# A fused attention and gated-MLP block: a new order for the first rows, maxima stored by ScalarE's queue, score tiles taken in turn, and scratch of q and k in two parts

## The chip, the cores and the metric

The kernel runs on one core of a Trainium2 chip. A core has five engines that run side by side, each with its own queue of instructions: TensorE (PE in the profile, its weight loads are PEld), VectorE (DVE), ScalarE (ACT), GpSimd (POOL) and SyncE (SP), which here only issues transfers (DMAs) between the chip's memory and SBUF. SP, ACT and POOL can all issue DMAs. Products go to PSUM, from which DVE and ACT read. The metric is the time of one execution in microseconds on the device; the kernel before took 1966.16 us (median of 3 runs, 1964.69 to 1969.37).

## The reference

With x of 2048 rows and 512 columns, all in float32:

```python
xn = layernorm(x)
qkv = xn @ wqkv                       # 32 heads of 16 columns
p = softmax(q @ k.T * 16 ** -0.5)     # for each head, 2048 x 2048
A = (p @ v) @ wo
z = gelu(xn @ w_in)                   # 2048 x 1792
z1, z2 = z[:, :896], layernorm(z[:, 896:])
B = (z1 * (w_sp @ z2 + b_sp)) @ w_out
out = x + A + B
```

## The kernel before

**Numbers in two parts.** Most operands are split into a high part (a copy in the type that PE reads at full rate, `F32R`) and a low part (the difference). `mm3` (L161) makes a product of three: high by high, low by high, high by low. `split` (L157) makes the parts of a psum tile, with a copy on ACT and a difference on DVE. `end` (L182) does so for weights: early weights get their high part by a second DMA that POOL issues (`begin`, L168, `early`) and the low part on DVE; later ones get both on POOL.

**The start** (L816 to L854). `load_x` (L223) loads four tiles of 128 rows of x as two transfers. `norm_x` (L233) normalises them: statistics on DVE, root and scaled copy on ACT. `turn_x` (L255) turns a group of four tiles with 16 transposes on PE into four column blocks, each in a psum tile of its own from `spsum` (L153), splits them and stores them to `xscr`. Then, for each of four groups of 512 rows, `qk_group` (L287) makes q and k of the first eight heads (m = 0, 12 products each), and `v_tile` (L334) makes v for four tiles, 12 products each. Between the v tiles, the next group is turned and the one after it normalised.

**Scratch of q and k.** The scores of a head use three products stacked in rows of one: q's parts high, low, high against k's high, high, low, each 16 rows. `qk_split` (L305) makes the parts of a projection; `qk_store` (L278) writes them to `qscr` or `kscr`, which hold three parts: one transfer of two parts (512 KB) and one of the repeated high part (256 KB). `load_stacks` (L598) then reads for a pair of heads the 48 rows of each head and side in one transfer, into `qst` and `kst`. The tile `hl` that the stores read has three buffers (L147). `store` goes by POOL's queue at the start and by SP's later (L134).

**The loop** (L943 to L1014). A step is one block of 128 keys for a pair of heads and 512 queries. A period of two half-steps has three steps. In each half-step the code writes, in order, the products of score tiles (`scores`, L898, for a step) and of maximum tiles (`max_mm`, L622, 27 steps ahead), the exponentials on ACT (`exp`, L920), the products with v (`pv`, L864), the maxima on DVE (`max_red`, L632), and pieces of the other work (the remaining q and k, then the MLP and the output), which generators hand out by a credit in PE time and estimated loads of the engines. Engines run what is written in that order. Score and maximum tiles both come from `spsum`: a ring of three psum buffers of two banks.

**The maxima.** Every 16 steps, `max_fin` (L640) ends a group: five small operations on DVE, the last a transpose into `ms`; then SP stores `ms` to `mscr` a half-step later (L659), and two half-steps later SP reads it back as four rows into `qst`, where it becomes a part of the scores' product. `later` (L125) puts a call off by so many half-steps; `flush` makes those that are due.

**The output of the MLP.** `mlp_out` (L565) loads for each tile of rows two pieces of the gated activation and one tile of x, one tile ahead.

Of the kernel before, what the change touches and what calls it, by code (L numbers as in the profile page):

```python
# [16 lines left out]
P = 128  # L17
# [3 lines left out]
DH = 16  # L21
# [10 lines left out]
RING = 20  # L32
LEAD = 27
# [6 lines left out]
def fused_block(ctx, tc, x, wqkv, wo, w_in, w_spT, b_sp, w_out, out):  # L40
# [39 lines left out]
    qscr = [dr.tile([P, 3, S], F32, name=f"qscr{m}") for m in range(4)]  # L80
    kscr = [dr.tile([P, 3, S], F32, name=f"kscr{m}") for m in range(4)]
# [45 lines left out]

    def flush():
        due = [l for l in late if l[0] <= now[0]]
        late[:] = [l for l in late if l[0] > now[0]]  # L130
        for _, fn, args in due:
            fn(*args)
# [19 lines left out]

    def spsum(nm):  # L153

        return ps.tile([P, 2, 512], F32, tag="s", name=nm, bufs=3)
# [12 lines left out]
    def begin(nm, src, n, blocks=1, t=None, early=None):  # L168
# [4 lines left out]
        dst, hi = rw[:, :n], t[:, 0, :n]  # L173
        if blocks > 1:
            src = src.rearrange("(c p) f -> p c f", p=P)
            dst, hi = (v.rearrange("p (c f) -> p c f", c=blocks) for v in (dst, hi))
        move(dst, src)
        if early:
            nc.gpsimd.dma_start(hi, src)
        return t, rw, n  # L180

    def end(loaded, early=False):  # L182
        t, rw, n = loaded
        if early:
            nc.vector.tensor_sub(t[:, 1, :n], rw[:, :n], t[:, 0, :n].bitcast(F32))
# [37 lines left out]
    def load_x(g):  # L223
        xt = [at.tile([P, 2, D], F32, tag="pf", name=f"x{g}_{i}", bufs=PF) for i in (0, 2)]
        for i in range(len(xt)):
            k = 4 // len(xt)
            t = 4 * g + k * i
            rows = x[t * P:(t + k) * P, :]
            move(xt[i], rows if k == 1 else rows.rearrange("(a p) d -> p a d", p=P))
            for j in range(k):  # L230
                xs[g, k * i + j] = xt[i] if k == 1 else xt[i][:, j, :]

    def norm_x(g, parts=1):  # L233
# [5 lines left out]
        for a in range(parts):  # L239
            tiles = range(a * k, (a + 1) * k)  # L240
            sl = slice(a * k, (a + 1) * k)
# [13 lines left out]
    def turn_x(g):  # L255
        for c in range(ND):
            pt = spsum(f"xT{g}_{c}")[:, 0, :]
            for i in range(4):
                nc.tensor.transpose(pt[:, i * P:(i + 1) * P], xs[g, i][:, c * P:(c + 1) * P], ident)
            t = piece(f"xnT{g}_{c}")  # L260
            split(t[:, 0, :], t[:, 1, :], pt, 512)
            store(xscr[g][c], t)
            xnT[g, c] = t
# [13 lines left out]

    def qk_store(scr, order, hl, sl, first=False):  # L278
        put = move if first else store
        r = 1 if order[0] == order[1] else 0  # L280
        put(scr[:, r:r + 2, sl], hl)
        put(scr[:, 2 - 2 * r, sl], hl[:, 0, :])
# [22 lines left out]
    def qk_split(m, g, a, src):  # L305
        hl = hilo(f"qkhl{m}_{a}_{g}")
        act(hl[:, 0, :], src, AF.Copy, 512)
        yield
        if m:
            gps(1.3).tensor_sub(hl[:, 1, :], src, hl[:, 0, :].bitcast(F32))  # L310
            yield from pool_done()
        else:
            dve(512).tensor_sub(hl[:, 1, :], src, hl[:, 0, :].bitcast(F32))
        qk_store((qscr, kscr)[a][m], ((0, 1, 0), (0, 0, 1))[a], hl, slice(g * 512, (g + 1) * 512), m == 0)
# [19 lines left out]
    def v_tile(t, ws):  # L334
        acc = dpsum(f"v{t}", "do"[t % 2])
        sl = slice((t % 4) * P, (t % 4 + 1) * P)
        for c in range(ND):
            xt = xnT[t // 4, c]
# [226 lines left out]
    def mlp_out():  # L565
        def load(t):
            hp = []
            for i, n in enumerate((4, 3)):
                h = piece(f"hp{t}_{i}")
                move(h[:, :, :n * P].rearrange("p a (f q) -> p a f q", q=P), hscr[t // 4][:, :, t % 4, 4 * i:4 * i + n, :])  # L570
                hp.append(h)
            xt = t512(f"xr{t}")
            move(xt, x[t * P:(t + 1) * P, :])
# [24 lines left out]
    def load_stacks(p, cols=slice(0, S)):  # L598
# [3 lines left out]
        for j in range(2):  # L602
            for i, (t, scr) in enumerate(((q, qscr), (k, kscr))):
                args = t[64 * j:64 * j + KS, cols], scr[m][sl[j], :, cols]
                if p and 2 * j + i:
                    later(2 * j + i, move, *args)
                else:
                    move(*args)
# [3 lines left out]
    NSTEP = NP * 64  # L612
    mstep = {}
# [26 lines left out]
    def max_fin(i):  # L640
# [18 lines left out]
        later(1, move, mscr[g % 4].rearrange("b k x -> (b k) x"), ms)  # L659
# [155 lines left out]
    with tc.manual_schedule(engines=engines):  # L815
        load_x(0)  # L816
        w0 = [begin(*qk_weights(0, a), early="t") for a in range(2)]
        load_x(1)
# [234 lines left out]
```

## Time and profile before

| | |
|---|---|
| median of 3 runs | 1966.16 us |
| lowest and highest | 1964.69, 1969.37 us |
| profiled execution | 1965.23 us, of which the span of instructions is 1963.1 us |
| PE busy | 1933.9 us (99%) |
| DVE busy | 1372.9 us (70%) |
| ACT busy | 1231.7 us (63%) |
| POOL busy | 720.9 us (37%) |
| scores, products with v, maxima (PE) | 445.6, 511.0, 446.9 us |
| maxima on DVE | 1024 of 1.222 us |
| exponentials on ACT | 1024 of 1.025 us |
| memory traffic | 190.09 MB read, 101.97 MB written |

The span runs from the first instruction to the last. PE's busy time is a model: products are pipelined, so where it says 99%, PE may still lose time between them. The table of a stretch gives, for each engine, busy time and the number of instructions in it. A timeline's line gives start, duration, engine, line of the code, operation, output and inputs, and in brackets how long the engine stood idle before and what ended that. DMA time is not shown on an engine; the queue that issues it is (SPq, POOLq).

### The profile page before, as it was taken

Reading aid. Unit: us, or ns where it says so; the run is one execution under the profiler, and the core shown is the slowest. Engines: PE = TensorE matmul, PEld = TensorE weight load, DVE = VectorE, ACT = ScalarE, POOL = GpSimd, SP = SyncE. Lnnn points to the kernel's source line nnn. Section 1 sums busy time; section 2 is a strip of 40 time slices with the busy share of each in tenths; the row PEclk is TensorE's granted clock in tenths of the full one; section 3 lists DMA queues with packets and bytes.
Section 4 is the critical chain, followed back from the end, with each engine's and each line's share of the span. In section 5 each row is a group of like instructions: output and inputs, shape, how many; then the busy total and the mean of one; then the engine's idle time right before and its main releaser. Section 6 shows DMA issues by size and latency. Waiting matters only on the chain.

```text
span 1963.1 us, 32545 instructions
## 1 busy us (share of the span) xinstructions
PE 1933.9 (99%) x12544; PEld 1047.0 (53%) x12544; DVE 1372.9 (70%) x1562; ACT 1231.7 (63%) x1402; POOL 720.9 (37%) x787
## 2 busy tenths in 40 slices
PE   7999999999999999999999999999999999999998
PEld 6765555555555555555555555555555555555543
DVE  5256777777777677777777777777777777777872
ACT  4336778888777665656666665665566655556664
POOL 2234368789776931026122531017112300002100
PEclk9999999999999999999999999999999999999999
DMA  9586444363535645365545744346364645355323
GB/s 327 204 292 200 139 107 122 108 176 111 154 117 159 187 123 140 91 162 159 151 138 154 211 129 125 108 126 204 105 163 135 176 142 145 106 152 154 105 73 113
DMA packets 234195, 294.20 MB, mean 150 GB/s; under 512 B 34536, under 2 KB 134520, under 8 KB 231160
## 3 DMA queue, kind: packets, MB, share of 16 engines
q1 hardware_dynamic: 229816, 282.08, 49.4%
q0 software_dynamic: 4224, 10.04, 1.4%
q8 instruction: 99, 1.62, 0.3%
q14 instruction: 56, 0.46, 0.1%
HBM read 190.09 MB, written 101.97 MB: 149 GB/s over the span
## 4 chain that ended last, share of the span: by engine, by line
PE 91%; DVE 3%; POOL 2%; DMA 2%; ACT 1%; issue 1%; SPq 0%; DVEq 0%; POOLq 0%; ACTq 0%
PE o L877 23%; PE mx L630 15%; PE st L903 15%; PE sp L162 7%; PE sp L164 5%; PE sp L163 5%; PE mo L162 2%; PE z1p L162 2%; PE qk L162 1%; DVE mm L638 1%; PE mo L163 1%; PE mo L164 1%; PE z2p L162 1%; PE z1p L164 1%; PE z1p L163 1%; PE qk L163 1%
## 5 line engine op out<-in xcount | busy, mean ns | idle before, releaser
L638 DVE TENSOR_REDUCE mm<-mx 128x2 f32<-128x1024 f32 x1024 | 1221.5, 1222 | 501.3 <-PE mx L630 497.2
L57 ACT ACTIVATE pf<-st 128x1024 f32<-128x1024 f32 x1024 | 1028.7, 1025 | 621.9 <-PE st L903 597.2
L877 PE MATMUL o<-pf,vall 128*32 128x512 f32 (+1 forms) x5120 | 511.0, 513 | 0.0
L630 PE MATMUL mx<-kst,qst 48*128 48x512 f32 x2048 | 446.9, 434 | 3.1 <-DVE mm L638 2.0
L903 PE MATMUL st<-qst,kst 50*128 50x512 f32 x2048 | 445.6, 432 | 1.5 <-DVE mm L638 1.4
L630 PEld LDWEIGHTS mx<-kst,qst 48*128 48x128 f32 x2048 | 192.0, 185 | 268.7 <-ACT pf L57 168.6
L903 PEld LDWEIGHTS st<-qst,kst 50*128 50x128 f32 x2048 | 193.3, 185 | 164.0 <-issue 85.7
L877 PEld LDWEIGHTS o<-pf,vall 128*32 128x32 f32 x5120 | 131.4, 109 | 233.7 <-issue 211.7
L162 PE MATMUL sp<-wsp,zs 128*128 128x512 f32 x448 | 193.8, 433 | 0.3 <-DVE z1i L549 0.2
L556 POOL TENSOR_TENSOR z1i<-z1i,hhl 128x512 f32<-128x512 f32 x28 | 36.0, 1286 | 425.9 <-DVE z1i L549 422.4
L164 PE MATMUL sp<-wsp,zs 128*128 128x512 f32 x448 | 175.9, 393 | 0.0
L163 PE MATMUL sp<-wsp,zs 128*128 128x512 f32 x448 | 175.9, 393 | 0.0
L162 PEld LDWEIGHTS sp<-wsp,zs 128*128 128x128 f32 x448 | 83.9, 187 | 68.9 <-issue 52.1
L164 PEld LDWEIGHTS sp<-wsp,zs 128*128 128x128 f32 x448 | 84.1, 188 | 19.3
L163 PEld LDWEIGHTS sp<-wsp,zs 128*128 128x128 f32 x448 | 84.4, 188 | 12.2
L187 POOL CAST wo<-wo0r 128x512 fp32r<-128x512 f32 x1 | 0.6, 611 | 191.4 <-DMA wo0r<-in_wo 191.4
L310 POOL TENSOR_TENSOR qkhl<-qr,qkhl 128x512 fp32r<-128x512 f32 x24 | 30.9, 1289 | 78.9 <-ACT qkhl L57 78.8
L162 PE MATMUL z2p<-w,xt 128*128 128x448 f32 x128 | 51.3, 401 | 0.0
L162 PE MATMUL mo<-wout,hp 128*128 128x512 f32 x112 | 48.5, 433 | 0.6 <-DVE xr L593 0.4
L691 POOL TENSOR_TENSOR ob<-ob 128x512 f32<-128x512 f32 (+1 forms) x16 | 20.6, 1288 | 77.0 <-DMA ob<-rscr 54.5
L164 PE MATMUL z2p<-w,xt 128*128 128x448 f32 x128 | 46.9, 366 | 0.0
L163 PE MATMUL z2p<-w,xt 128*128 128x448 f32 x128 | 46.8, 365 | 0.0
(378 smaller groups left out, 1974.8 us busy)
## 6 DMA issues: line engine op xcount, KB each, us to landing
zs<-z2scr SPq DMA_DIRECT2D x112, 512.0 KB
escr<-e SPq DMA_DIRECT2D x60, 256.0 KB
hscr<-hhl SPq DMA_DIRECT2D x28, 512.0 KB
qst<-qscr SPq DMA_DIRECT2D x30, 384.0 KB
kst<-kscr SPq DMA_DIRECT2D x30, 384.0 KB
xscr<-xnT POOLq DMA_DIRECT2D x16, 512.0 KB, 6.0
qscr<-qkhl SPq DMA_DIRECT2D x16, 512.0 KB
kscr<-qkhl SPq DMA_DIRECT2D x16, 512.0 KB
```

Source lines behind the costliest of these rows:

```text
L57: return nc.scalar.activation(out, in_, func, **kw)
L162: nc.tensor.matmul(acc, lh, rh, start=first, stop=False)
L163: nc.tensor.matmul(acc, ll, rh, start=False, stop=False)
L164: nc.tensor.matmul(acc, lh, rl, start=False, stop=last)
L187: gps(0.6).tensor_copy(t[:, 0, :n], rw[:, :n])
L310: gps(1.3).tensor_sub(hl[:, 1, :], src, hl[:, 0, :].bitcast(F32))
L556: gps(1.3).tensor_add(z1, z1, hl[:, 1, :].bitcast(F32))
L630: nc.tensor.matmul(acc[:, j, :], qst[p % 2][rows, tt * P:(tt + 1) * P], kst[p % 2][rows, kc * 512:(kc + 1) * 512], start=True, stop=True)
L638: dve(1024).tensor_reduce(mmax[i // 16][:, :, t, kc], mstep.pop(i), AX.X, ALU.max)
L691: gps(1.3).tensor_mul(both[rows, 0, :], both[rows, 0, :], both[rows, 2, :])
L877: nc.tensor.matmul(acc[cols:cols + VW, a:a + w], vpack(kt - 1 + r, 2 * p + j), pf[:, j * 512 + a:j * 512 + a + w], start=(kt == 1 and a == ...
L903: nc.tensor.matmul(st[:, j, :], kst[p % 2][rows, kt * P:(kt + 1) * P], qst[p % 2][rows, c * 512:(c + 1) * 512], start=True, stop=True)
```

## The change

- **Start.** x's first group comes as four transfers, two tiles first, then the four blocks of v's weights, then the other two tiles, then the weights of q and k. The second DMAs of early weights are gone: POOL casts the high parts of v's weights, DVE makes three low parts and POOL the fourth; POOL makes both parts of the first weights of q and k. A group's turning can be done for two tiles of four: the first two tiles are turned, v is made for them, then the other two, v again, and only then q and k of this group. All of a group's transposes are written first, into three psum tiles of which one holds two column blocks, and the splits behind them. ACT takes a root of a constant before anything else. Fifteen products of zeros (`WARM`) are written on PE ahead of all others. Group 1 is normalised between the v tiles of group 0 and turned between its q and its k.
- **Maxima.** The store of `ms` is put in a list, `behind`, and issued by ACT's queue at the end of the next half-step, behind its exponentials.
- **Score tiles.** `spsum` takes three tiles with one buffer each in turn, where it had one tag with three buffers.
- **Scratch.** `qscr` and `kscr` hold two parts. For k the order of the parts is low, high. One store writes both; `load_stacks` reads the two parts as 32 rows and the high part again as 16 rows, eight transfers where there were four.
- **Output of the MLP.** From the second tile on, the three loads are put off by one, two and three half-steps.

```diff
-    qscr = [dr.tile([P, 3, S], F32, name=f"qscr{m}") for m in range(4)]
-    kscr = [dr.tile([P, 3, S], F32, name=f"kscr{m}") for m in range(4)]
+    qscr = [dr.tile([P, 2, S], F32, name=f"qscr{m}") for m in range(4)]
+    kscr = [dr.tile([P, 2, S], F32, name=f"kscr{m}") for m in range(4)]
...
+    def soon(k, fn, *args):
+        fn(*args)
+
...
     def spsum(nm):
-        return ps.tile([P, 2, 512], F32, tag="s", name=nm, bufs=3)
+        turns[0] += 1
+        return ps.tile([P, 2, 512], F32, tag=f"s{turns[0] % 3}", name=nm, bufs=1)
...
-    def end(loaded, early=False):
+    def end(loaded, low=None, high=False):
         t, rw, n = loaded
-        if early:
-            nc.vector.tensor_sub(t[:, 1, :n], rw[:, :n], t[:, 0, :n].bitcast(F32))
+        if high:
+            low.tensor_sub(t[:, 1, :n], rw[:, :n], t[:, 0, :n].bitcast(F32))
+        elif low:
+            nc.scalar.activation(t[:, 0, :n], rw[:, :n], AF.Copy)
+            low.tensor_sub(t[:, 1, :n], rw[:, :n], t[:, 0, :n].bitcast(F32))
         else:
             gps(0.6).tensor_copy(t[:, 0, :n], rw[:, :n])
...
-    def turn_x(g):
+    def turn_x(g, lo=0, hi=4):
+        tiles = [spsum(f"xT{g}_{lo}_{c}") for c in range(3)]
+        sl = slice(lo * P, hi * P)
         for c in range(ND):
-            pt = spsum(f"xT{g}_{c}")[:, 0, :]
-            for i in range(4):
-                nc.tensor.transpose(pt[:, i * P:(i + 1) * P], xs[g, i][:, c * P:(c + 1) * P], ident)
-            t = piece(f"xnT{g}_{c}")
-            split(t[:, 0, :], t[:, 1, :], pt, 512)
-            store(xscr[g][c], t)
-            xnT[g, c] = t
+            for i in range(lo, hi):
+                nc.tensor.transpose(tiles[c % 3][:, c // 3, i * P:(i + 1) * P], xs[g, i][:, c * P:(c + 1) * P], ident)
+        for c in range(ND):
+            if lo == 0:
+                xnT[g, c] = piece(f"xnT{g}_{c}")
+            t = xnT[g, c]
+            split(t[:, 0, sl], t[:, 1, sl], tiles[c % 3][:, c // 3, sl], (hi - lo) * P)
+            if hi == 4:
+                store(xscr[g][c], t)
...
-    def qk_store(scr, order, hl, sl, first=False):
-        put = move if first else store
-        r = 1 if order[0] == order[1] else 0
-        put(scr[:, r:r + 2, sl], hl)
-        put(scr[:, 2 - 2 * r, sl], hl[:, 0, :])
...
-        qk_store((qscr, kscr)[a][m], ((0, 1, 0), (0, 0, 1))[a], hl, slice(g * 512, (g + 1) * 512), m == 0)
+        (store if m else move)((qscr, kscr)[a][m][:, :, g * 512:(g + 1) * 512], hl)
...
-                move(h[:, :, :n * P].rearrange("p a (f q) -> p a f q", q=P), hscr[t // 4][:, :, t % 4, 4 * i:4 * i + n, :])
+                (later if t else soon)(i + 1, move, h[:, :, :n * P].rearrange("p a (f q) -> p a f q", q=P), hscr[t // 4][:, :, t % 4, 4 * i:4 * i + n, :])
...
-            move(xt, x[t * P:(t + 1) * P, :])
+            (later if t else soon)(3, move, xt, x[t * P:(t + 1) * P, :])
...
-                args = t[64 * j:64 * j + KS, cols], scr[m][sl[j], :, cols]
-                if p and 2 * j + i:
-                    later(2 * j + i, move, *args)
-                else:
-                    move(*args)
+                two = t[64 * j:64 * j + 2 * DH, cols], scr[m][sl[j], :, cols]
+                one = t[64 * j + 2 * DH:64 * j + KS, cols], scr[m][sl[j], i, cols]
+                for args in (two, one):
+                    if p and 2 * j + i:
+                        later(2 * j + i, move, *args)
+                    else:
+                        move(*args)
...
-        later(1, move, mscr[g % 4].rearrange("b k x -> (b k) x"), ms)
+        behind.append((now[0] + 1, mscr[g % 4].rearrange("b k x -> (b k) x"), ms))
...
+        nc.scalar.activation(mhalf, epst, AF.Sqrt)
+        idle = piece("idle")
+        nc.vector.memset(idle.bitcast(F32)[:, 0, :], 0.0)
+        nc.vector.memset(mhalf, -0.5)
+        rest = dpsum("idle", "o")
+        for _ in range(WARM):
+            nc.tensor.matmul(rest, idle[:, 0, 0:P], idle[:, 0, :], start=True, stop=True)
...
+        for t, rw, n in wv:
+            nc.gpsimd.tensor_copy(t[:, 0, :], rw)
+        norm = norm_x(0, 2)
+        next(norm)
+        next(norm)
+        wv = [end(l, (nc.vector, nc.gpsimd)[c == 3], True) for c, l in enumerate(wv)]
+        turn_x(0, 0, 2)
+        next(norm)
...
+        w0 = [end(l) for l in w0]
+        run(norm)
+        v_tile(0, wv)
+        v_tile(1, wv)
+        turn_x(0, 2, 4)
+        norm1 = norm_x(1, 2)
+        next(norm1)
+        v_tile(2, wv)
+        next(norm1)
+        next(norm1)
+        v_tile(3, wv)
+        run(norm1)
...
             for n in ns[1:]:
                 exp(n)
+            while behind and behind[0][0] <= half:
+                nc.scalar.dma_start(*behind.pop(0)[1:])
```

## The prediction

> **What bounds the kernel now.** I read the page's busy shares first, then busy time by stretch, then the timeline of the first 14 us and of one step in the main loop.
>
> ```profile
> PE 1933.9 (99%) x12544; PEld 1047.0 (53%) x12544; DVE 1372.9 (70%) x1562; ACT 1231.7 (63%) x1402; POOL 720.9 (37%) x787
> ```
>
> PE is the bound; a change that adds no matmul to its crowded part can gain only where PE stands idle. Where is that? By stretch (columns: busy time and count of PE, PEld, DVE, ACT, POOL; granted clock; DMA share; GB/s):
>
> ```profile
> 0.00:13.90 13.90, 4.38 (x17) 3.42 (x18) 6.94 (x21) 6.71 (x10) 6.68 (x16) 1.00 1.02 294
> 13.90:88.00 74.10, 72.10 (x339) 58.97 (x337) 27.15 (x58) 30.11 (x53) 14.17 (x24) 1.00 0.76 281
> 88.00:143.90 55.90, 53.48 (x234) 36.80 (x232) 32.71 (x32) 18.40 (x30) 24.94 (x22) 1.00 0.71 256
> 143.90:146.90 3.00, 1.92 (x13) 0.97 (x12) 1.58 (x2) 2.40 (x3) 0.06 (x1) 1.00 0.96 354
> 146.90:150.40 3.50, 3.50 (x12) 2.29 (x12) 2.00 (x2) 1.57 (x3) 1.29 (x1) 0.52 0.35 132
> 150.40:1900.00 1749.60, 1745.79 (x11564) 921.08 (x11564) 1280.25 (x1422) 1140.44 (x1270) 672.85 (x723) 1.00 0.50 142
> 1900.00:1963.10 63.10, 52.73 (x380) 23.45 (x372) 22.23 (x28) 32.04 (x36) 0.92 (x2) 0.94 0.26 89
> ```
>
> Of 29.2 us idle, 9.5 lie before 13.9, 2.0 in the projections, 3.5 between 88 and 147, 3.8 in the whole loop, and 10.4 in the tail, which the change leaves alone. At 146.9 to 150.4 the clock is half: a stall costs twice. The start in detail:
>
> ```profile
> 4.54 0.69 DVE L244 BATCH_NORM_STATS2 bst<-x 128x6 f32<-128x512 f32 x1 [3.46 <-DMA x<-in_x]
> ...
> 7.01 1.52 ACT L253 ACTIVATE x<-x,rs 128x512 f32<-128x512 f32 x2 [0.43 <-DVE rs L249]
> ...
> 9.34 1.52 ACT L253 ACTIVATE x<-x,rs 128x512 f32<-128x512 f32 x2 [0.43 <-DVE rs L249]
> ...
> 10.91 3.04 PE L259 MATMUL xT<-ident,x 128*128 128x128 f32 x13 [0.23 <-ACT x L253]
> ...
> 13.60 0.63 PE L162 MATMUL qk<-xnT,wqk 128*128 128x512 f32 x1
> ```
>
> The first product waits for all four tiles of x to be normalised and turned. The thirteen transposes follow each other every 0.213 us (2.56 us over twelve steps). Later ones take half of that:
>
> ```profile
> 44.39 1.47 PE L259 MATMUL xT<-ident,x 128*128 128x128 f32 x12
> 46.45 0.66 PE L259 MATMUL xT<-ident,x 128*128 128x128 f32 x4 [0.59 <-DVE xnT L159]
> ```
>
> Twelve in 1.47 us, the last lasting 0.27: 0.109 us apart. The last four wait for a psum buffer that VectorE still reads.
>
> **The change, part by part.** I sum against the profiled execution: 1965.23 us (span 1963.1), 0.93 under the median of 1966.16.
>
> *Start.* Now: 12 products at 0.2267 us make a group of 2.72 us; the first maximum is at 87.76, and 13.60 + 0.24 (first product late) + 24 groups (65.3) + 48 transposes (5.2) + about 3.4 of gaps comes to 87.7. After the change x comes tile by tile, the value weights next, and a product needs two tiles only. Two tiles of x are the 512 KB of the first old transfer (statistics at 4.54 at the latest; the first tile half a transfer earlier, about 3.9). Statistics 0.69 and 0.66 with aggregates, root, reciprocal and offset took 2.47 from 4.54 to ACT's 7.01; from 3.9 that gives 6.4, and 1.52 more is 7.9. The added root on ACT (0.30 behind the table load that ends at 2.00) and VectorE's memset behind it are done by 2.5, under the wait for x. Eight transposes at 0.109 follow. The split is now of 256 columns: ACT between 512 (0.60) and 256 (0.39 in the tail's 256-column copies), VectorE about 0.42 (0.425 for its 256-column copy). The first product comes 0.52 + 0.39 after 7.9 (0.52 is 10.91 to 11.43), at 8.8, its second one 0.42 later: in effect a stream from 9.0. The weights: six transfers of 0.26 MB at 294 to 380 GB/s land by 5.3 to 6.2; POOL's casts (0.61 x 4) end by 8 and VectorE's three differences (0.69 each) by 9, before each is used. So the stream starts 13.84 - 9.0 = 4.8 us earlier.
>
> Against that: the other eight transposes of the group now stand in the stream (0.87), and the third tile's first products wait for their split (0.55: ACT first empties v1, 0.60, then 0.39 and 0.42). The turning of groups 1 to 3 loses its gaps, since four half tiles lie in three buffers: 0.28 + 0.54 at 25 to 27.5, 0.59 at 46.45, the same again at 65: 2.0, and 0.13 us for each restart. Inserting group 1's transposes after the first q group may wait 0.3 for its last normalised tile. Start, net: 4.8 - 0.87 - 0.55 - 0.3 + 2.0 + 0.4 + the small early stall at 19.46 (0.15) = 5.6; bounds 3.5 (weights or x later by 2) and 7.3 (first x as early as 3.4, no waits).
>
> *The products of zeros.* Fifteen of 512 columns start when a 128x512 memset is done (about 1.6). At the half-clock spacing of 0.427 (147.53 to 149.24) they end at 8.0, at 0.227 at 5.0: before the transposes, or 0.1 into them. They buy the clock for 8 + 8 transposes and the first products.
>
> **A rule for the clock.** The row: after 2.6 us of transposes the product at 14.07 is already followed at 0.23, and after stops of 1.55 and 1.08 us within ten us the clock halves for 3.4 us. The Trainium skill (TensorE: Matmul & The Clock Gate, Part 1: The HAM clock gate) says that the array runs at half rate until a window of about 3.4 us, free-running, has been busy, and falls back after an idle one. The halved rows agree with it; by it the zeros (busy from 1.6 for 3.4 to 6.4 us) do open the gate, but whether it stays open over the pause before 7.9 depends on where the window lies, which is a rival below. The page's Part 4 says that transposes do not open the gate; 10.91 to 14.07 speaks against it.
>
> *q and k scratch.* 32 stores of 256 KB go (32 issues of about 0.45 on SP); each stack load becomes two, 4 more issues of 0.42 for each of 19 loads of stacks (76 x 0.42 = 32 us of SP's queue). SP is idle for hundreds of us in waits, and a stack is asked for over 40 us ahead; no PE wait on a stack shows. The bytes read stay. What it frees is the stretch where the stores hold up PE:
>
> ```profile
> 136.18 0.63 ACT L57 ACTIVATE qkhl<-qr 128x512 fp32r<-128x512 f32 x1 [7.16 <-DMA kscr<-qkhl]
> ...
> 137.35 0.50 PE L162 MATMUL qk<-xnT__1182,wqk 128*128 128x512 f32 x1 [1.55 <-ACT qr L57]
> ```
>
> ACT waits for a buffer whose two stores (768 KB, DMA share 1.05) are not done. Five stores in flight lose a third, 1.3 MB or 3.3 us at 400 GB/s: I take the 1.55 as gone. What is late next is the maximum at 146.00 (1.08, VectorE); I leave that and the halved 3.4 us (worth 1.7) in place. So 1.5; bounds 0 and 1.55 + 1.08 + 1.7 = 4.3.
>
> *Maxima by ACT's queue.* 64 issues leave SP (0.33 each) and wait on ACT for VectorE's transpose, behind the odd half-step's exponential:
>
> ```profile
> 1012.10 0.21 DVE L657 STREAM_TRANSPOSE ms<-mrow 128x32 f32<-128x32 f32 x1
> ...
> 1012.75 1.02 ACT L57 ACTIVATE pf<-st 128x1024 f32<-128x1024 f32 x1 [0.63 <-PE st L903]
> 1015.67 1.02 ACT L57 ACTIVATE pf<-st 128x1024 f32<-128x1024 f32 x1 [1.90 <-PE st L903]
> ```
>
> The transpose ends at 1012.31, the exponential at 1013.77, ACT then rests until 1015.67. Read group by group, the transpose has ended first in all 63 groups of the loop, and in 54 ACT then rests 0.56 us or more; in the other nine another ACT piece of the MLP follows and comes 0.33 later. No trace shows an issue on ACT: between SP's 0.33 and POOL's 0.57 (cscr). I take 0.4, hidden by that rest; on the path 0, bounds -1 (SP's queue moves sooner) and +9 x 0.57 = 5. Queued behind it on ACT are the next exponentials, which PE needs one half-step (2.7 us) later. The store lands some 1.5 us later, against 12 steps or 22 us until its rows are read.
>
> *Score tiles in turn.* At 1006.86 and 1007.55 the waits already are those of a ring taken in turn (first maximum after the first exponential, second after the second). Worth 0; bounds -3.8 (all of the loop's idle time) and +1.
>
> *Late loads of the output stage.* One half-step to three later (2.7 to 8 us) against 14 us between load (1615.80) and first use (1631.34): 0.
>
> Sum: 5.6 + 1.5 = 7.1, so 1965.2 - 7.1 = 1958.1, or 1959 from the median. I say 1958.5.
>
> **Rivals.**
> Middle freed: the earlier stores also clear the 146.00 stall, and with it the halved clock: 2.8 more, and with the first x at 3.4 another 0.5: 1955. For it: both stalls lie 9 us apart in one chain of ACT. Against: the second is a wait for VectorE's maxima.
> Cold again: the gate closes in the pause after the zeros, so 16 transposes cost 0.10 more each and up to 3.4 us of products half their speed (1.7), or x comes at 4.5: 3.3 lost, 1962. For: stops of 1.1 to 1.6 did it at 147. Against: the stop at 135.7 to 137.35 alone did not.
> Slower: ACT's queue. If an issue is not 0.4 but waits for ACT's pipeline or for the transpose, the following exponential and then PE's maximum that takes its buffer come late. From 7.1 / 63 = 0.11 us per group on PE's path the gain is gone; at 0.2 us it is 1971, and at 0.33 (every issue fully exposed, 21 us) 1980. For it: in the stretch 250 to 500 ACT is 80% busy. Against: the rests above.
> Given back: the loop's own pacing or late stacks eat the start: 1965.
>
> **Numbers.** A measurement tells about 0.2% (3.9 us). Main case 1958.5 (1956 to 1961): 0.50. Middle freed, 1955: 0.18. Cold again, 1962: 0.16. Given back, 1965: 0.08. ACT's queue, 1970 or more: 0.08. Faster: the first two and most of the third, 0.82; same 0.10; slower 0.08. The range of 8 in 10 leaves out the last two cases: 1953 to 1963.
>
> **What would show it.** First v product near 8.8 to 9.2, first maximum near 82; transposes 0.109 apart in the first ten us (0.213 if the gate was shut); no gap inside a group's sixteen transposes; no wait of ACT for kscr near 130; in the loop no ACT wait for VectorE's ms and 3.8 us or less of PE idle. Wrong if the loop from its first score to 1900 takes longer than before, or if the first product is later than 11.

## The result and the profile after

The changed kernel takes 1958.18 us (median of 6 runs, 1957.26 to 1960.21) against 1966.19 us of the kernel before (6 runs, 1964.69 to 1969.64), run beside it: a ratio of 0.996 with a 95% interval of 0.995 to 0.997. Forecast were 1958.5 us and a range of 1953 to 1963. The profiled execution of the changed kernel is the slowest of its six (1960.21, span 1958.44), so the two profiles stand only 5.0 us apart (1965.23 and 1960.21), and the medians 8.0.

The page's busy shares of the changed kernel:

```profile
PE 1938.7 (99%) x12559; PEld 1049.7 (54%) x12559; DVE 1373.7 (70%) x1565; ACT 1232.5 (63%) x1407; POOL 725.5 (37%) x790
```

PE idles 19.8 us instead of 29.2. Of the 9.4 us saved, 5.2 are now filled by the fifteen products of zeros, and the rest is nearly the difference of the spans (4.64). By stretch (length, then busy time and count of PE, PEld, DVE, ACT, POOL; granted clock, DMA share, GB/s), cut where the changed kernel's own stages end:

```profile
0.00:10.00 10.00, 6.98 (x24) 4.93 (x24) 4.84 (x15) 4.24 (x8) 3.79 (x10) 1.00 0.81 255
10.00:15.10 5.10, 3.99 (x11) 3.13 (x12) 4.63 (x11) 0.68 (x2) 4.93 (x7) 0.67 1.07 377
15.10:85.90 70.80, 69.95 (x334) 57.68 (x332) 25.00 (x57) 32.04 (x57) 16.45 (x27) 1.00 0.63 230
85.90:140.40 54.50, 53.62 (x235) 36.98 (x234) 32.73 (x32) 18.75 (x30) 25.35 (x22) 1.00 0.64 219
140.40:144.40 4.00, 3.33 (x17) 1.82 (x17) 3.00 (x3) 3.33 (x6) 0.26 (x2) 1.00 0.35 132
144.40:1895.00 1750.60, 1746.91 (x11564) 921.53 (x11562) 1280.91 (x1422) 1140.97 (x1271) 673.80 (x724) 1.00 0.49 140
1895.00:1958.40 63.40, 53.89 (x384) 23.60 (x380) 22.60 (x28) 32.51 (x36) 0.92 (x2) 0.94 0.26 88
```

The stretch at half clock that lay behind the first scores is gone. Another stands at the start: 10.0 to 15.1 has a granted clock of 0.67, since it is halved from 11.7 to 15.1. The projections idle 0.85 us instead of 2.0, the stretch up to the first scores 0.88 instead of 2.4, the loop 3.7 instead of 3.8.

Five points of the timeline, in us from the start, show where the time went. The later rows are kernels of the experiments.

| kernel | first maximum | first score | 13th exponential | last exponential | span |
|---|---|---|---|---|---|
| before | 87.76 | 143.94 | 166.2 | 1947.8 | 1963.08 |
| after | 85.91 | 140.44 | 161.2 | 1943.0 | 1958.44 |
| after, maxima by SP | 84.30 | 138.87 | 159.6 | 1942.1 | 1956.60 |
| after, three parts of scratch | 84.06 | 140.95 | 163.2 | 1944.6 | 1959.93 |
| before, changed start alone | 83.10 | 138.91 | 160.1 | 1942.2 | 1958.24 |
| before, scratch in two parts alone | 87.95 | 142.53 | 163.3 | 1951.8 | 1966.43 |
| before, strict turn alone | 88.71 | 144.98 | 167.1 | 1949.4 | 1964.64 |
| after, score tiles from one ring | 85.62 | 140.15 | 160.9 | 1950.5 | 1966.21 |
| after, ring and three parts | 83.40 | 142.38 | 163.1 | 1944.5 | 1960.76 |
| after, value tiles in pairs | 83.87 | 138.45 | 159.2 | 1941.1 | 1955.84 |

From before to after, 1.85 us are won up to the first maximum and 3.15 more up to the thirteenth exponential; from there to the last exponential both take the same, 1781.6 and 1781.8 us, and the tail behind it stays (15.3 and 15.4).

The start of the changed kernel, from its timeline (start, duration, engine, line, operation; in brackets the idle time before and what ended it):

```profile
1.54 5.23 PE L842 MATMUL idle<-idle 128*128 128x512 f32 x15 [1.54 <-DVE idle L838]
...
6.80 0.61 POOL L857 CAST qst<-wv0r 128x512 fp32r<-128x512 f32 x1 [5.50 <-DMA wv0r<-in_wqkv]
...
7.43 0.98 PE L276 MATMUL xT<-ident,x 128*128 128x128 f32 x7 [0.31 <-ACT x L268]
7.44 0.69 DVE L191 TENSOR_TENSOR qst<-wv0r,qst 128x512 fp32r<-128x512 f32 x1 [1.62 <-POOL qst L857]
7.51 1.09 POOL L857 CAST qst<-wv1r 128x512 fp32r<-128x512 f32 x1
...
8.64 1.07 DVE L191 TENSOR_TENSOR qst<-wv1r,qst 128x512 fp32r<-128x512 f32 x1 [0.51 <-POOL qst L857]
...
8.98 0.47 PE L170 MATMUL v<-qst,xnT 128*128 128x512 f32 x1 [0.56 <-ACT xnT L58]
...
9.63 1.09 DVE L191 TENSOR_TENSOR kst<-wv2r,kst 128x512 fp32r<-128x512 f32 x1
...
10.64 1.40 DVE L167 TENSOR_TENSOR xnT<-xT,xnT 128x256 fp32r<-128x256 f32 x4
...
11.11 0.50 PE L171 MATMUL v<-qst,xnT 128*128 128x512 f32 x1 [1.65 <-DVE xnT L167]
```

The first product stands at 8.98 (before: the first of q and k at 13.60). The second, which multiplies the low part of x, comes only at 11.11. That low part is made by VectorE at 10.64, behind three differences of the weights, and each of these waits for POOL's cast of the same piece. The first piece has landed only at 6.80. Casts and differences also hold each other up: a cast takes 0.61 us at 6.80 and 1.09 at 7.51, beside the difference of 7.44; a difference takes 0.69 at 7.44 and 1.07 at 8.64. Shortly after the stop of 1.65 us the clock halves for 3.4 us.

The stop of 1.55 us at 137.35 is gone. The timeline at the place that answers to it:

```profile
132.69 0.63 ACT L58 ACTIVATE qkhl<-qr 128x512 fp32r<-128x512 f32 x1 [5.51 <-DMA kscr<-qkhl]
...
133.89 0.50 PE L170 MATMUL qk<-xnT__1212,wqk 128*128 128x512 f32 x1
```

ACT still waits for the store of k, but it goes on at 132.69, and PE's next product (133.89) follows without a gap.

The store of the maxima on ACT, from the view of the tile ms (durations in ns as lowest/median/highest, then who waited, in us and times):

```profile
L1024 ACTq DMA_DIRECT2D mscr<-ms x64: 325/326/341, 115.2 to 1903.6; - x64
...
  ACT pf L58: 3.5, 2
```

All 64 issues cost 0.33 us each, and two exponentials out of 1024 are put down to a wait for them, 3.5 us together.

### The profile page after: what moved, and what is told of

Same layout as the page of the kernel before. It is cut to its first block, busy times and chain, and to the rows that moved or that the text cites. A ratio compares the mean times of both kernels' runs of the same rounds, so it can differ in the third digit from the quotient of the medians.

```text
span 1958.4 us, 32641 instructions
## 1 busy us (share of the span) xinstructions
PE 1938.7 (99%) x12559; PEld 1049.7 (54%) x12559; DVE 1373.7 (70%) x1565; ACT 1232.5 (63%) x1407; POOL 725.5 (37%) x790
## 3 DMA queue, kind: packets, MB, share of 16 engines
q8 instruction: 99, 1.62, 0.3%
## 4 chain that ended last, share of the span: by engine, by line
PE 95%; DVE 2%; ACT 1%; issue 1%; DMA 0%; POOL 0%; SPq 0%; DVEq 0%; ACTq 0%
PE o L929 23%; PE mx L650 16%; PE st L955 15%; PE sp L170 7%; PE sp L172 5%; PE sp L171 5%; PE mo L170 2%; PE qk L170 2%; PE z1p L170 2%; PE z2p L170 2%; PE qk L171 1%; PE qk L172 1%; PE mo L171 1%; PE mo L172 1%; PE z1p L172 1%; PE z1p L171 1%
```

## The experiments

My theory was the sum of the prediction: most of the gain from the start, some from fewer stored bytes, nothing from the rest. The rivals: the zeros carry the start (the clock); the gain in the middle comes from taking the maxima off SP's queue; the turn of the score tiles matters. I took parts back out of the changed kernel one at a time, put parts alone into the kernel before, made one suspected cost four times as frequent, and mended the stop at 11.11. Ratios are to runs of the kernel before in the same group of runs.

**1. Without the products of zeros**

```diff
-        for _ in range(WARM):
-            nc.tensor.matmul(rest, idle[:, 0, 0:P], idle[:, 0, :], start=True, stop=True)
```

> The changed kernel without its fifteen products of zeros and their psum tile. Theory (the zeros open the clock early, but do not hold it through the pause before the second v product): the first eight transposes stand 0.21 us apart instead of 0.11 (+0.8 us at most, under the wait for the split), and the v products run at half speed for up to one window of 3.4 us whether or not zeros came before. First maximum 0 to 2 us later than with zeros, time 1958 to 1960.5. Rival (the zeros carry the gain at the start): first maximum at 88 or later, time 1961 or more.

Measured: 1959.92 us (1959.41 to 1960.65), 0.9969 (0.9956 to 0.9981), 1.7 above the changed kernel. PE's timeline without the zeros:

```profile
7.53 1.76 PE L276 MATMUL xT<-ident,x 128*128 128x128 f32 x7 [0.17 <-ACT x L268]
9.85 0.77 PE L170 MATMUL v<-qst,xnT 128*128 128x512 f32 x1 [0.56 <-ACT xnT L58]
```

Seven transposes take 1.76 us instead of 0.98 (0.22 us apart instead of 0.12, with the last taking 0.45 or 0.27), and the products stay at 0.43 us apart until the clock opens at 15.1. The 1.7 us lie within the spread of the two intervals, but the profiles agree with them: the first maximum is at 85.68 without the zeros, and at 83.79 and 84.06 with them in experiments 7 and 2, where POOL's first cast of the weights starts at nearly the same time (5.80; 5.71 and 6.00). So the zeros are worth 1.6 to 1.9 us here, inside the 0 to 2 that were expected; they do not carry the start.

**2. Three parts of scratch again**

```diff
-    qscr = [dr.tile([P, 2, S], F32, name=f"qscr{m}") for m in range(4)]
-    kscr = [dr.tile([P, 2, S], F32, name=f"kscr{m}") for m in range(4)]
+    qscr = [dr.tile([P, 3, S], F32, name=f"qscr{m}") for m in range(4)]
+    kscr = [dr.tile([P, 3, S], F32, name=f"kscr{m}") for m in range(4)]
...
-                for args in (two, one):
+                for args in ((t[64 * j:64 * j + KS, cols], scr[m][sl[j], :, cols]),):
```

In this run alone k's three parts stood in another order, so that its scores are sums of other products of parts and it does not compute the reference; instructions and bytes are the same, and experiment 11 has the parts in their right order.

> The changed kernel with scratch of q and k back in three parts, the high part stored twice and each stack read by one transfer. Theory (fewer stored bytes free the buffers of the parts between 88 and 150 us): ACT again waits 5 us or more for the store of k near 130, PE stops 1 to 2 us near 135 to 138, the step from the first maximum to the first score grows by 1 to 2.5 us, time 1959.5 to 1962. Rival (the stall went because the store of the maxima left SP's queue): no such wait, time 1958 within 1 us.

Measured: 1960.35 us (1958.79 to 1962.22), 0.9971 (0.996 to 0.9982), 2.2 above the changed kernel. Its timeline:

```profile
133.22 0.63 ACT L58 ACTIVATE qkhl<-qr 128x512 fp32r<-128x512 f32 x1 [7.83 <-DMA kscr<-qkhl]
...
134.38 0.50 PE L170 MATMUL qk<-xnT__1211,wqk 128*128 128x512 f32 x1 [1.80 <-ACT qr L58]
```

The stop is back with 1.80 us, and with it a clock halved from 144.0 to 147.4. From the first maximum to the thirteenth exponential the kernel takes 79.1 us against 75.3 of the changed one: 3.8 us. That stretch takes 75.3 us in eight of the nine profiles with scratch in two parts, whatever else differs (76.5 in experiment 7). With three parts it takes 77.0 in experiment 5, where the clock stays full, and 78.4 to 79.7 in the four profiles in which it halves. The maxima were off SP here too, so the rival of the middle falls: the scratch did it. Whether by its fewer bytes or by its fewer transfers is not separated.

**3. The maxima by SP's queue again**

```diff
-        behind.append((now[0] + 1, mscr[g % 4].rearrange("b k x -> (b k) x"), ms))
+        later(1, move, mscr[g % 4].rearrange("b k x -> (b k) x"), ms)
```

> The changed kernel with the store of the maxima issued by SP again. Theory (the store costs nothing on ACT and gains nothing elsewhere): the distance from the first maximum to the last exponential stays within 0.5 us, time 1958 within 1 us. Rival one (SP's queue was what held up the stores near 130): the stop near 137 returns, +1.5 us. Rival two (ACT pays for the issues, which is where 0.9 us went between the 300th and the 860th exponential): 0.5 to 1.5 us faster.

Measured: 1958.31 us (1956.67 to 1958.78), 0.9957 (0.9943 to 0.997). The queue makes no difference that can be measured, and no stop near 137 returns. At the start the stop at the second product is 1.07 us instead of 1.65, the clock does not halve behind it, and the first maximum is at 84.30.

**4. The first two value tiles made together**

```diff
-        v_tile(0, wv)
-        v_tile(1, wv)
+        v_pair(0, wv)
...
+    def v_pair(t, ws):
...
+        todo = [(0, 0, c, j) for c in range(ND) for j in range(2)]
+        todo += [(1, 0, c, j) for c in range(ND) for j in range(2)]
+        todo += [(0, 1, c, j) for j in range(2) for c in range(ND)]
+        for a, b, c, j in todo:
+            nc.tensor.matmul(acc[j], xnT[t // 4, c][:, a, sl[j]], ws[c][:, b, :], ...)
...
```

and VectorE makes one weight's difference ahead of the low parts of x, the other two behind.

> The changed kernel with the first two v tiles made together: all high by high products of both tiles first, then low by high, then high by low; on VectorE the low parts of x stand behind the first weight difference instead of behind three. The same products are made. Theory (PE stopped 1.65 us at the second v product because VectorE had three weight differences ahead of the low part of x, and that stop shut the clock for 3.4 us): no stop over 0.6 us after the first v product, no half clock between 8 and 20 us, first maximum 2.5 to 3.7 us earlier than the 85.9 of the changed kernel's profile, time 1954 to 1956. Rival (the weights themselves come too late): PE stops again, first maximum within 1 us of 85.9.

Measured: 1957.98 us (1957.61 to 1961.59), 0.996 (0.9947 to 0.9972); profiled span 1955.84. Its timeline:

```profile
9.19 1.42 DVE L167 TENSOR_TENSOR xnT<-xT,xnT 128x256 fp32r<-128x256 f32 x4 [1.83 <-ACT xnT L58]
9.30 1.17 PE L367 MATMUL v<-qst,xnT 128*128 128x512 f32 x4 [0.56 <-ACT xnT L58]
```

VectorE now makes the low parts at 9.19, and PE goes from product to product. The first maximum comes 2.0 us earlier than in the profile of the changed kernel, which is less than forecast, and the median does not move, where 1954 to 1956 were expected. Experiment 5 bears on why.

**5. The changed start alone**

The kernel before with the new order of its first 70 us (zeros, x by tiles, value weights first, half groups of transposes); scratch in three parts, maxima by SP, the ring and the undelayed loads as before. The diff is the change's own, less these four.

> Only the start of the change: scratch in three parts with its second stores, maxima stored by SP, the ring of three score tiles and the undelayed loads are those of before. Theory (start and stores are two gains that add; the others are worth nothing): first maximum at 84.1, or at 85.9 where the clock halves near 12 us, so 1.9 to 3.7 us earlier than before; from there to the 13th exponential 78 to 79 us as before, with the stop of 1.5 to 1.8 us near 135; time 1961.5 to 1964. Rival (the start alone carries the change, the rest of the gain is the clock's phase): 1958 to 1960.

Measured: 1960.56 us (1959.12 to 1962.82, 11 runs), 0.9976 (0.9967 to 0.9984): about 5 us of the 8. It was faster than expected. Its first maximum is at 83.10, 4.66 earlier than before and 2.81 earlier than in the profile of the changed kernel, for the most part because the stop behind the first product is missing here, with the same code. What differs is when the first piece of the value weights lands. Over all the profiles with exactly this start, POOL's first cast (which begins when the piece is there) and the second product go together:

| kernel | first cast, us | second product, us | stop before it, us |
|---|---|---|---|
| ring and three parts (11) | 5.36 | 9.67 | 0.05 |
| four issues (7) | 5.71 | 10.03 | 0.06 |
| start alone (5) | 5.72 | 9.88 | 0 |
| three parts (2) | 6.00 | 10.31 | 0.40 |
| maxima by SP (3) | 6.25 | 10.57 | 1.07 |
| ring (6) | 6.52 | 10.84 | 1.32 |
| changed kernel | 6.80 | 11.11 | 1.65 |

The transfer is issued at 1.64 to 1.66 in all; its landing differs by up to 1.4 us from run to run. The second product comes 4.31 or 4.32 us behind the first cast in all but the start alone (4.16). That chain is one cast, three differences and the first low part of x: at 0.61 and 0.69 throughout it would take about 0.61 + 3 x 0.69 + 0.47 = 3.15 us, so by this estimate the mutual hold-up makes the second product 1.2 us later, whenever the piece lands. Only the last two kernels have a clock halved behind the stop; from the second product to the first maximum they take 74.8 us, the others 73.2 to 73.8. The pair of experiment 4 should mend what happens in the late runs, but its own profile had an earlier landing (6.03), where little is to be won, so this is not shown. Only profiled executions have a timeline, so how often the late case comes is not known. The granted clock of a whole execution gives a hint: it is 0.997 in the profiled one of the changed kernel and 0.998 or 0.999 in its other five, and a halved stretch of 3.4 us lowers it by about 0.001.

**6. Score tiles from one ring of three buffers again**

```diff
-        turns[0] += 1
-        return ps.tile([P, 2, 512], F32, tag=f"s{turns[0] % 3}", name=nm, bufs=1)
+        return ps.tile([P, 2, 512], F32, tag="s", name=nm, bufs=3)
```

> The changed kernel with one tag and three buffers for score tiles again. Theory (the ring was already taken in turn nearly always): nothing, time 1957.5 to 1959, from the 49th to the 1001st exponential 1680.3 within 0.5 us. Rival (the strict turn is what lost or gained in the loop): that distance changes by 1 us or more.

Measured: 1969.69 us (1966.31 to 1975.9, 10 runs), 1.0022 (1.0012 to 1.0032): slower than the kernel before, and 11.5 above the changed kernel. This expectation was wrong. The timeline at one of five such places:

```profile
747.77 0.40 PE L649 MATMUL mx<-kst,qst 48*128 48x512 f32 x2
...
748.21 1.23 DVE L657 TENSOR_REDUCE mm<-mx 128x2 f32<-128x1024 f32 x1 [1.04 <-PE mx L649]
749.49 0.50 PE L954 MATMUL st<-qst,kst 50*128 50x512 f32 x2 [1.32 <-DVE mm L657]
```

The score tile at 749.49 is handed the very buffer in which the maxima of 747.77 were written, so it waits until VectorE has reduced them, 1.32 us in which nothing else is ready on PE. Which buffer a tile gets is settled when the program is built. In the built program the ring hands out one buffer twice running in five places; in the kernel before in none. The profile has five stops of 1.18 to 1.32 us, and from the thirteenth to the last exponential it takes 1789.6 us instead of 1781.8: 1.6 per stop. That is 7.8 us, as far as the two profiles stand apart, while the medians differ by 11.5. That goes with the clock: over the ten executions the mean granted clock falls from 0.998 in the fastest (1966.31) to 0.992 in the slowest (1975.9), so in the slower ones it was halved for longer.

**7. The store of the maxima by ACT in four issues**

```diff
-        behind.append((now[0] + 1, mscr[g % 4].rearrange("b k x -> (b k) x"), ms))
+        for u in range(4):
+            behind.append((now[0] + 1, mscr[g % 4][u], ms[32 * u:32 * u + 32, :]))
```

> The changed kernel with each store of the maxima cut into four of 32 rows, all by ACT's queue: three more issues per group, 1 us at 0.33 each. Theory (ACT rests 1.2 us or more behind the exponential in most groups, so issues there are hidden): 0 to 4 us slower, time 1958 to 1962. Rival (each issue reaches PE): 63 times 1 us, time 2010 or more.

Measured: 1974.48 us (1970.64 to 1976.77), 1.0044 (1.0027 to 1.0061), 16 above the changed kernel: also a miss. ACT's waits (what waited, what for: us in total, times, longest):

```profile
ACT pf L58 <- DMA mscr<-ms: 45.0, 26, 3.5
```

The exponentials wait 45 us for these stores, in 26 places, where the changed kernel shows 3.5 us in two. From the first to the last of a group's four issues ACT is taken for 1.73 us in the median group, more than many of its rests, and in some groups two successive issues begin far apart (at 1122.60, 1124.25, 1124.91 and 1126.62 in one; 4.5 us apart in another). What ACT waits for between them is not shown. So the cost that the prediction named as its slower rival exists with four issues; with a single one none can be measured.

**8. Both halves in pairs, statistics of the third and fourth tile ahead**

Against the kernel of experiment 4:

```diff
         w0v = end(wv[0], nc.vector, True)
+        next(norm)
         turn_x(0, 0, 2)
...
-        next(norm)
...
-        v_tile(2, wv)
         next(norm1)
         next(norm1)
-        v_tile(3, wv)
+        v_pair(2, wv)
         run(norm1)
```

> The kernel with the first two v tiles made together, and also the third and fourth; the statistics of the third and fourth tile of x stand ahead of the splits of the first two on VectorE. Theory (PE's stops of 0.38 and 0.37 at 15 to 16 us are waits for the normalised third and fourth tile, whose statistics stood behind the weight differences, and the 0.47 at 17.6 is the wait for a low part): the first two go, the third halves, first maximum at 82.6 to 83.2, time 1956 to 1957.5. Rival (the third and fourth tile of x arrive too late, and hold up the splits): first maximum at 84 or later.

Measured: 1959.07 us (1958.47 to 1959.52), 0.9967 (0.9955 to 0.9979): no better than the changed kernel, first maximum at 84.46. VectorE's timeline:

```profile
9.10 0.70 DVE L259 BATCH_NORM_STATS2 bst<-x 128x6 f32<-128x512 f32 x1 [2.29 <-DMA x<-in_x]
...
10.72 1.39 DVE L167 TENSOR_TENSOR xnT<-xT,xnT 128x256 fp32r<-128x256 f32 x4
```

The statistics wait 2.29 us for a tile of x, and the low parts of x stand behind them: 10.72 instead of 9.19. The rival held.

**9. Scratch in two parts alone.** After experiment 6 it was open which part of the change upsets the ring. This puts the scratch alone into the kernel before:

```diff
-    qscr = [dr.tile([P, 3, S], F32, name=f"qscr{m}") for m in range(4)]
+    qscr = [dr.tile([P, 2, S], F32, name=f"qscr{m}") for m in range(4)]
...
-                args = t[64 * j:64 * j + KS, cols], scr[m][sl[j], :, cols]
+                two = t[64 * j:64 * j + 2 * DH, cols], scr[m][sl[j], :, cols]
+                one = t[64 * j + 2 * DH:64 * j + KS, cols], scr[m][sl[j], i, cols]
...
```

> The kernel before with one part of the change alone: scratch of q and k in two parts, their high rows read twice; the score tiles still come from one ring of three buffers. Theory (the issues added by the second reads shift the planner's order of the ring's buffers, so that now and then one buffer is handed out twice running, as in the changed kernel with the ring): the stop of 1.55 us near 137 goes (2 to 4 us won), but four places of the loop show a PE stop of 1.2 to 1.4 us on VectorE's mm, with 1.5 to 2 us lost at each: 1967 to 1972 us in all, first score some 2 us earlier than before. Rival (the ring was upset by ACT's issue of the maxima or by the late loads, or by the changed start): no such stops in the loop, and the gain of the scratch alone is seen, 1963 to 1964.

Measured: 1970.13 us (1968.2 to 1975.49), 1.0035 (1.0021 to 1.0049). Up to the thirteenth exponential it is 3.0 us ahead of the kernel before; the stop near 137 is gone, and so is the halved clock. From there to the last exponential it takes 1788.5 us instead of 1781.6. PE's waits:

```profile
PE st L905 <- DVE mm L640: 4.1, 7, 1.3
PE mx L632 <- ACT pf L57: 3.5, 8, 1.2
```

The timeline has four stops of 1.32, 1.32, 1.18 and 1.18 us, at 197.2, 752.0, 1448.2 and 1788.9. The built program has four places with one buffer twice running. In the changed kernel the same two waits are small:

```profile
PE mx L650 <- ACT pf L58: 1.8, 7, 0.7
...
PE st L955 <- DVE mm L658: 1.1, 4, 0.4
```

**10. Strict turn alone, in the kernel before.** The edit is that of experiment 6 the other way round.

> The kernel before with one part of the change alone: score tiles taken strictly in turn from three tags of one buffer. Theory (the ring of before is in turn in 321 of its 338 periods and never hands out one buffer twice running, so a strict turn has nothing to win): 1965.5 to 1967 us, the loop as long as before within 1 us. Rival (each of the 17 periods out of turn makes PE wait): up to the loop's 3.8 us of idle time won, 1962.4 to 1964.

Measured: 1965.46 us (1963.82 to 1969.41, 10 runs), 1.0004 (0.9995 to 1.0014). Alone the turn wins nothing.

**11. One ring and three parts of scratch together.** Both edits of 2 and 6 in the changed kernel, k's parts in their right order.

> The changed kernel with two parts taken back together: the score tiles come from one ring of three buffers again, and q and k keep three parts of scratch, read once; the maxima still go by ACT's queue, and the late loads stay. Theory (only the scratch in two parts upsets the ring's order): no stops of 1.2 to 1.4 us in the loop, 1959 to 1962 us as with three parts and strict turn (1960.35). Rival (ACT's issue of the maxima or the late loads upset it): stops as in the changed kernel with the ring, 1968 to 1971.

Measured: 1960.53 us (1959.53 to 1962.51, 10 runs), 0.9979 (0.997 to 0.9989), the same as with three parts and strict turn (experiment 2). The long stops in the loop are gone; PE's waits:

```profile
PE st L955 <- DVE mm L658: 1.4, 5, 0.4
PE mx L650 <- ACT pf L58: 1.2, 6, 0.2
```

So the scratch in two parts, and neither ACT's issue nor the late loads, upsets the ring. It takes 32 stores away and adds 76 reads to the issues among which the work is dealt out; which of the two does it is not separated. This kernel differs from the start alone (experiment 5) only by ACT's issue and the late loads, and 0.9979 against 0.9976 shows these two to be worth nothing together that can be measured (each interval reaches 2 us to either side).

**12. The pair with the maxima by SP**

The edits of 3 and 4 together, as the candidate for a better version.

> The best of both: the changed kernel with the first two value tiles made together (products of high by high parts first, VectorE's low parts of x behind one weight difference) and the maxima by SP's queue. Theory (the pair keeps PE busy behind the first product, the queue of the maxima costs nothing either way): first maximum at 83.5 to 84.5, 1957.0 to 1958.5 us. Rival (SP's queue delays stacks once PE runs earlier): 1959 to 1962, with PE waiting on a stack's DMA.

Measured: 1957.82 us (1956.77 to 1963.73), 0.9969 (0.9956 to 0.9982); first maximum 83.21, span 1955.77, the shortest of all. By the medians it can't be told from the changed kernel. No version beats it measurably.

## Why the prediction came out right, and which of its steps did not

The total came within 0.3 us of the median, for the most part for the stated reasons. That it came so close is in part luck: two terms missed in opposite directions, and one dependence between two parts was not seen, which did no harm only because the change holds both of them.

- **Start: 5.6 forecast, about 5 measured.** Alone it has a ratio of 0.9976: 4.7 us by the ratio, 5.2 by the medians of its group of runs (1960.56 and 1965.74). The first product came at 8.98, inside the forecast of 8.8 to 9.2 (over the ten profiles with the zeros it came at 8.98 to 9.51). The step that failed is "VectorE's three differences (0.69 each) by 9, before each is used": they ended at 10.72. The first weights landed only at 6.80, where the prediction had all of them by 6.2, cast and difference held each other up, and the low parts of x stood queued behind them, so the second product came at 11.11 and not 0.42 after the first. With an early landing this stop is nearly zero, with the late one of the profile 1.65 us. The first maximum, forecast at about 82, came between 83.10 and 85.91. The bounds of 3.5 to 7.3 hold the measured value.
- **Products of zeros: as forecast in the profile of the changed kernel, not in every one.** Transposes stand 0.12 us apart with them and 0.22 without; their end at 6.77 lies between the two ends given. But in five of the ten profiles with zeros the clock opened only at 6.5 to 7.5. There the zeros ran on to 7.5 to 8.0 while the first tile of x was normalised by 6.8 to 7.2, and the first product came at 9.25 to 9.51: the zeros can stand in the way of the transposes by more than the 0.1 us that was allowed. The rival "cold again" did occur, in the profiled execution: the clock opened at 4.8 and halved from 11.7 to 15.1, but behind the stop at 11.11, not in the pause that I had named.
- **Scratch: 1.5 forecast, 2.2 by the medians and 3.8 by the profiles (experiment 2); within the bounds of 0 to 4.3.** The ratios of experiments 5 and 11 against that of the changed kernel put it at 3.1 and 3.7. The stop went as said; of the nine profiles with two parts only that of experiment 7 has one left, of 1.01 us. The step that failed is "I leave that and the halved 3.4 us (worth 1.7) in place". The halved clock went with the stop near 137, while the stop of 1.08 us behind the first scores can stay: it is still there in experiments 6 and 9, with a full clock. It is 1.08 in all five profiles with one ring and 0.66 or 0.67 in all nine with the strict turn, so the turn takes 0.4 us off it. So the rival "middle freed" came true in its effect and not by its mechanism.
- **Score tiles in turn: 0 forecast, and 0 measured alone (experiment 10); beside the scratch 11.5 us (experiment 6).** The prediction read the ring of the kernel before, which was in order, and took it that the order would stay so. It priced the scratch's 76 issues on SP's queue and asked nothing else of them. Without the turn the scratch alone is a loss of 0.35%. The two parts belong together, and only as a pair do they have a price.
- **Maxima by ACT: 0 forecast, 0 measured.** The issue costs 0.33 us instead of the 0.4 that was taken, and only two exponentials are put down to a wait for one. Experiment 7 shows that the rival was no idle thought: four issues in a row cost 16 us.
- **Late loads: 0 forecast.** They were not tried alone; together with ACT's issue they are worth nothing that can be measured (experiments 5 and 11).
- **What was to be seen.** No wait of ACT for VectorE's ms, and 3.7 us of idle time in the loop: right. "No gap inside a group's sixteen transposes" was wrong twice: 0.31 at 7.43 and 0.37 at 44.45, both for a tile of x not yet normalised. "No wait of ACT for kscr near 130" was wrong too: ACT still waits 5.51 us for it until 132.69; what went is PE's stop behind that wait.

Start and scratch with its turn sum to 5.2 + 2.2 = 7.4 of the measured 8.0; the rest lies within the intervals.

## What to carry to other kernels

When a change adds or removes instructions that a planner deals out among others, ask what else takes its order from that: here a scratch tensor written and read in other pieces made a ring hand out the same psum buffer twice running, 1.6 to 1.7 us each time, and a fixed turn that is worth nothing by itself paid for all of it. Take each part out of the changed kernel and also put it alone into the old one; a part that shows nothing in one of the two may decide in the other. In a start, put on each queue what the next product needs ahead of what later products need, and look at several profiles, since a landing that shifts by a microsecond decides which of them waits.

## What the runs showed of the hardware

- **VectorE and POOL block each other.** A cast on POOL takes 0.61 us alone and 1.09 while VectorE subtracts one tile in SBUF from another; VectorE's subtraction takes 0.69 alone and 1.07 or 1.09 when a cast has begun before it. The first to start keeps its own time, and the second ends some 0.5 us after it; so the second waits, and the two do not run slower side by side. The Trainium skill (SBUF — State Buffer, SBUF: two separate sides) says that an operation of VectorE with two inputs in SBUF and a GpSimd operation that reads SBUF take one shared port pair as an exclusive lock. The trace agrees, by these numbers; the prediction had reckoned 0.61 and 0.69 throughout.
- **The clock can fall some time after a stop.** In the middle of the kernel the clock was halved in all four profiles with a stop of 1.55 us or more near 135 (1.55 before; 1.62, 1.76 and 1.80 in experiments 10, 11 and 2), for 3.4 us each time. It began 0.7 us after that stop in experiment 11 and 9.6 to 10.0 us after it in the other three, 1.1 to 1.8 us behind the stop at the first scores. In the profiles whose longest stop there was 1.16 us or less it was never halved, not even with stops of 1.16 and 1.08 (experiment 5). The Trainium skill (TensorE: Matmul & The Clock Gate, Part 1: The HAM clock gate) has the clock fall back after an idle window of about 3.4 us. The length of the halved stretch agrees; but no stop there was longer than 1.80 us, and yet the clock fell. In the loop, stops of 1.32 us left it full in the profiles of experiments 6 and 9, while in experiment 7 it halved behind stops of 1.54 and 2.38 us, for 3.4 and 6.8 us. Within each profile its changes lie whole multiples of 3.413 us apart (in the kernel before 133.12 us are 39 of them and 1805.65 us are 529). What share of idle time closes the gate, and over how long, these runs do not settle.
- **A few issues of DMAs on ACT are not a multiple of one.** One store per group by ACT cost nothing that can be measured, four cost 16 us, with successive issues of one group up to 4.5 us apart.
